# The order of the delta rule planned with TensorE's full-clock durations, and filler products in TensorE's planned gaps

## The chip, the core and the metric

The kernel runs on one core of a Trainium2 chip. The metric is device time in microseconds of one execution, lower is better: 908.51 us for the kernel before, the median of three runs (907.62 to 911.17).

## What is computed

Two blocks follow each other. The first is a delta rule over 4 batches, 8 heads and 768 tokens with a head dimension of 48; its output is reshaped to 3072 tokens of 384 numbers. The second routes each token to two of eight experts by noisy logits, and runs the experts.

```python
    k_n = k / (np.linalg.norm(k, axis=-1, keepdims=True) + 1e-06)
    for t in range(S):
        kt, vt, bt = (k_n[:, :, t], v[:, :, t], beta[:, :, t, None])
        y[:, :, t] = np.einsum('bhd,bhde->bhe', q[:, :, t], state)
        v_old = np.einsum('bhde,bhd->bhe', state, kt)
        state = state + bt[:, :, :, None] * np.einsum('bhd,bhe->bhde', kt, vt - v_old)
...
    noisy_logits = logits + noise_scale * noise
    top2 = np.argpartition(-noisy_logits, 2, axis=1)[:, :2]
...
            h = np.maximum(x[mask] @ w1[e], 0.0)
            out[mask] += top2_w[mask, k, None] * (h @ w2[e])
```

## The kernel before

The delta rule is computed in chunks of 64 tokens (`C`). A unit is one chunk of two batches, so that its 128 rows fill the partitions; there are 12 chunks of 2 units each. Four units (two chunks) make a round, and there are six rounds. In a round the kernel does this, by job:

- `turned` (L477) transposes k and later q of a unit on TensorE, four transposes to a job (L484), and ScalarE copies the result out of PSUM (L491). `products` (L508) then makes the Gram matrix of k (L502, the helper `by_token`), whose diagonal blocks are copied to `gd` (L531) and whose other part to `at` (L537).
- `invert` (L541) inverts the triangular blocks of all units of the round on VectorE: a transposition (L548), row lengths through ScalarE (L555 to L569), the scaling by `low_d` (made by GpSimd, L584, save in the first round), then 30 columns of two dependent instructions each (L599, L603), and the transposed inverses `tb` (L624) and `tt` (L630). It is one long chain of VectorE instructions.
- `join` (L634) puts the 32-wide blocks together on TensorE (L671, L677), with copies on ScalarE (L651, L685, L689).
- `within` (L700) makes the masked product of q and k (L502, then L713 on VectorE).
- `recur` (L720) is the recurrence proper: the state times k (L502, `pair<-st,kT`), subtracted from v on VectorE (L751), solved with the joined inverse (L761), copied by ScalarE (L768), multiplied with k (L779) and added to the state on VectorE (L791). GpSimd scales v (L732) and spreads the state (L804).
- `answer` (L811) makes the outputs (L823, L834), transposes them (L843) and multiplies them with the router's weights (L848). `route` (L894) chooses the experts on VectorE (L906 and around; L955 to L961 count on TensorE, L975 makes the gates, L983 counts), and GpSimd writes each token's row to the rows of its two experts in DRAM (L325).

What sets the order of all this is the class `Jobs`. Each piece of work is a job with an engine and a cost in microseconds, what it reads and writes, and, for TensorE, a PSUM bank that it opens. `order` (L84) first gives every job a due time backwards from its followers, with their costs and 0.15 us for a signal; then it plays the queue of each engine forward in planned time, starting the job that can start first, and among those within 0.05 us of it the one with the earliest due time. A job that opens a bank waits for the earliest empty one (`place`, L105; `empty` holds the planned time at which each bank comes free). The jobs are then emitted in the order of their planned starts; for TensorE, ScalarE, VectorE and SyncE this order is kept as it is. So a cost changes no instruction, only places in the queues. The times of the plan itself exist only while the kernel is built.

`early` (L1073) adds the first part of expert 0's work at the end of the delta rule (L1131, L1157, L1180), as jobs that are taken when nothing else is due. After that the experts run in an order of their own, which no cost touches: the rest of expert 0 (`rest`, L1559) and experts 1 to 7 (L1628, products at L1408).

Of the kernel before, what the change touches and what calls it, by code (L numbers as in the profile page):

```python
# [38 lines left out]
class Jobs:  # L39
# [44 lines left out]
    def order(self):  # L84
        jobs = self.jobs
        for job in reversed(jobs):
            for i in job.after:
                jobs[i].due = min(jobs[i].due, job.due - job.cost - self.SIGNAL)
        for job in jobs:
            job.key = (0, job.due) if job.late is None else (1, job.late)  # L90
        waits = [len(job.after) for job in jobs]
        then = [[] for _ in jobs]
        for job in jobs:
            for i in job.after:
                then[i].append(job.number)
        ready = [0.0] * len(jobs)
        could = [set() for _ in self.ENGINES]
        for job in jobs:
            if not job.after:
                could[job.engine].add(job.number)  # L100
        free = [0.0] * len(self.ENGINES)
        empty = {size: [0.0] * len(x) for size, x in self.banks.items()}
        spaced = moved = 0.0

        def place(size, among):  # L105

            return min(
                ((empty[size][i], i) for i in among if empty[size][i] is not None),
                default=None,
            )  # L110

        done = []
        while len(done) < len(jobs):
            first = {}
            best = None
            for engine in self.ENGINES:
                at = []
                for i in could[engine]:
                    start = max(free[engine], ready[i], spaced if jobs[i].apart else 0.0)
                    if jobs[i].opens:  # L120
                        which = jobs[i].opens.size, jobs[i].opens.among
                        if which not in first:
                            first[which] = place(*which)
                        room = first[which]
                        if room is None:
                            continue
                        start = max(start, room[0])
                    at.append((start, jobs[i].key, i))
                if at:
                    soon = min(at)[0] + self.PATIENCE  # L130
                    pick = min((x for x in at if x[0] <= soon), key=lambda x: x[1:])
                    best = min(best or (1e9,), pick)
            start, _, i = best
            job = jobs[i]
            could[job.engine].remove(i)
            end = free[job.engine] = start + job.cost
            if job.apart:
                spaced = start + job.apart
            if job.opens:
                size, among = job.opens.size, job.opens.among  # L140
                job.opens.at = x = first[size, among][1]
                empty[size][x] = None
                job.opens.tile = self.banks[size][x]
            if job.closes:
                empty[job.closes.size][job.closes.at] = end + self.SIGNAL
            job.start = start
            if job.moves:
                end = moved = max(moved, end) + job.moves
            done.append(job)
            for j in then[i]:  # L150
                ready[j] = max(
                    ready[j],
                    end + (self.SIGNAL + job.lands if jobs[j].engine != job.engine else 0.0),
                )
                waits[j] -= 1
                if not waits[j]:
                    could[jobs[j].engine].add(j)
        return sorted(done, key=lambda job: job.start)

    PATIENCE = 0.05  # L160

    def run(self):
        for job in self.order():
            job.emit()

@with_exitstack
def kernel(
# [39 lines left out]
    nc = tc.nc  # L207
# [165 lines left out]
    def deltanet(ictx):  # L373
# [8 lines left out]
        PE, ACT, DVE, POOL, SP = Jobs.ENGINES  # L382
# [91 lines left out]
        def halves(name, slot):  # L474
            return [(name, slot, i) for i in range(2)]

        def turned(n, name, src, size, to, to_size):  # L477

            p = bank(1, True)

            def emit():
                p_t = p.tile.rearrange("p (j t) -> p j t", t=128)
                for j in range(NP):
                    nc.tensor.transpose(p_t[:, j], src(n)[:, 2 * j : 2 * j + 2], ident)  # L484

            jobs.add(
                PE, 0.75, emit, reads=halves(name, n % size), opens=p,
            )
            jobs.add(
                ACT, 0.6,  # L490
                lambda: nc.scalar.copy(  # L491
                    to(n), p.tile.rearrange("p (j t) -> p j t", t=128)
                ),
                writes=[(name + "T", n % to_size)], closes=p,
            )
# [12 lines left out]
        def products(n):  # L508

            s, i = divmod(n, US)
            turned(n, "k", kps, NK, kTs, NT_)
            p = bank(2, True)
            jobs.add(
                PE, 0.8,
                lambda: by_token(
                    two_banks(p, C), kTs(n), lambda z, j, b: kTs(n)[z, j, rows_of[b]]
                ),  # L520
                reads=[("kT", n % NT_)], opens=p,
            )
            gd = gds.rearrange("p (u j z) i -> p u z j i", u=US, z=2)[:, i]
            for x, lo in enumerate(range(0, 128, Q)):
                rows, cols = slice(lo, lo + Q), slice(lo % C, lo % C + Q)
                on, copy = (DVE, nc.vector.tensor_copy) if s == 0 and x % 2 else (
                    ACT, nc.scalar.copy
                )
                jobs.add(
                    on, 0.38,  # L530
                    lambda rows=rows, cols=cols, copy=copy: copy(  # L531
                        gd[rows], two_banks(p, C)[rows, :, :, cols]
                    ),
                    writes=[("gd", i, lo)], uses=p,
                )
            jobs.add(
                ACT, 0.38, lambda: nc.scalar.copy(ats(n), two_banks(p, C)[:, :, :, Q:C]),  # L537
                writes=[("at", n % NT_)], closes=p,
            )
# [94 lines left out]
        def join(units):  # L634
# [21 lines left out]
            for n, m in zip([*units, None], [None, *units]):  # L656
# [31 lines left out]
                    for up, dn in pairs:  # L688
                        nc.scalar.copy(w64s(m)[up, :, Q:C], p_x()[up])  # L689

                jobs.add(PE, 1.25, products_of, reads=reads, opens=p)
                if n is not None:
                    jobs.add(
                        ACT, 0.8, negated, writes=[("x", n % 2)],
# [5 lines left out]
        def within(n):  # L700

            turned(n, "q", qps, NQ, qTs, NQ)
            p = bank(2, True)
            jobs.add(
                PE, 0.8,
                lambda: by_token(
                    two_banks(p, C), kTs(n), lambda z, j, b: qTs(n)[z, j, rows_of[b]]
                ),
                reads=[("kT", n % NT_), ("qT", n % NQ)], opens=p, lands=2.0,
            )  # L710
            jobs.add(
                DVE, 0.7,
                lambda: nc.vector.tensor_tensor(  # L713
                    out=qks(n), in0=two_banks(p, C),
                    in1=mask[:, None, None, :].to_broadcast([128, 2, NP, C]), op=ALU.mult,
                ),
                writes=[("qk", n % NQ)], closes=p,
            )

        def recur(n):  # L720
# [18 lines left out]
            if c:  # L739
                p_b = bank(2)  # L740
                jobs.add(
                    PE, 0.7,
                    lambda: by_token(
                        two_banks(p_b, D), kTs(n), lambda r, j, b: old[r, b, j]
                    ),
# [17 lines left out]
                            start=(h == 0), stop=(h == H - 1), skip_group_check=True,  # L763
                        )

            jobs.add(PE, 1.3, solve, reads=[*v_key, *every_w], opens=p_u)
            jobs.add(
                ACT, 0.5, lambda: nc.scalar.copy(u_n, per_head(p_u)),  # L768
                writes=[u_key], closes=p_u,
# [5 lines left out]
            def gather_state():  # L775
# [7 lines left out]
                            )  # L783

            jobs.add(
                PE, 0.7, gather_state, reads=[u_key, *halves("k", n % NK)], opens=p_s
            )

            def add_state():
# [21 lines left out]
        def answer(n):  # L811
# [41 lines left out]
            reads = [("qT", n % NQ), ("qk", n % NQ), ("u", n % N_U)]  # L853
            if c:
                reads.append(("wide", z, c % 2))
            jobs.add(PE, 2.2 if c else 1.3, of_chunk, reads=reads, opens=p_y)
            jobs.add(
                ACT, 0.5,
                lambda: nc.scalar.copy(y_n, per_head(p_y).rearrange("p h d -> p (h d)")),
                writes=[y_key], closes=p_y,  # L860
            )
            jobs.add(PE, 0.6, turn, reads=[y_key], opens=p_xt)
            jobs.add(
                ACT, 0.5,
                lambda: nc.scalar.copy(
# [1 line left out]
                ),  # L867
                writes=[xT_key], uses=p_xt,
            )
            jobs.add(PE, 1.0, multiply, reads=[xT_key, "wgn"], uses=p_xt)  # L870
            jobs.add(
                ACT, 0.2,
                lambda: nc.scalar.copy(
# [404 lines left out]
                cut(s, EARLY[s][1] * 128)  # L1278
        for s in EARLY:
            early(s)  # L1280
        with tc.manual_schedule(
            engines={
                mybir.EngineType.PE, mybir.EngineType.Activation, mybir.EngineType.DVE,
                mybir.EngineType.SP,
            }
        ):
            jobs.run()
        return held["w"]

    with ExitStack() as ictx:  # L1290
# [14 lines left out]
    with ExitStack() as ectx:  # L1305
# [322 lines left out]
        for e in range(1, E):  # L1628
# [32 lines left out]
            def run(g, *numbers):  # L1661
                for n in numbers:
                    steps[g][n - 1]()
# [143 lines left out]
```

## Time and profile before

| | us |
|---|---|
| median of three runs | 908.51 |
| the profiled execution | 894.65 |
| its span | 892.8 |
| TensorE busy in the span | 790.1 |
| VectorE busy | 504.7 |
| first inversion starts (L548) | 16.0 |
| first expert product of 512 columns (L1157) | 354.0 |
| last product of the early part of expert 0 (L1180) | 408 |

The profile is of one execution, so durations and places are those of the 894.65 us, not of the median. The page cuts the span into 40 slices; a digit is the busy share of a slice in tenths, and for the line PEclk the granted share of TensorE's full clock. A matmul of float32 appears as two records, one after the other; a transposition as one. Each wait is put down to the event that ended it; "issue" means that the profile shows nothing that the engine waited for.

### The profile page before, as it was taken

The numbers are of one execution on the slowest core, as the hardware profiler recorded it, in microseconds if no ns is written. First come the engines' busy times: TensorE is split into PE (matmuls) and PEld (weight loads), VectorE is DVE, ScalarE is ACT, GpSimd is POOL, SyncE is SP. The second block draws the span as 40 slices with busy tenths as digits, with TensorE's granted clock in tenths as the row PEclk, the third lists the DMA queues.
The fourth block names the chain that finished last, engine by engine and source line by source line (L and its number), as shares of the span: only waits on it lengthen the run. The fifth ranks groups of instructions, "written<-read, shape, count | busy, mean of one in ns | idle before, by whom it ended". The sixth has DMA issues, their size and how long they took to land. (4 is left out here: it accounts for less than half of the span.)

```text
span 892.8 us, 21764 instructions
## 1 busy us (share of the span) xinstructions
PE 790.1 (88%) x9170; PEld 607.4 (68%) x9170; DVE 504.7 (57%) x1210; ACT 311.5 (35%) x743; POOL 321.2 (36%) x331
## 2 busy tenths in 40 slices
PE   4569697697968879999999999999999999999995
PEld 3458585686848767467469578578578587587594
DVE  6968888785898961115465344444455344354342
ACT  3565636628457363201330330320330420420410
POOL 4031144224423323315423634614614515525311
PEclk8657687776976879999999999999999999999998
DMA  4698645451621212633612422423413322301201
GB/s 71 119 312 171 128 92 184 109 156 56 189 73 39 77 45 75 220 105 137 191 66 100 141 73 96 142 72 103 132 71 110 123 71 84 95 10 39 64 20 40
DMA packets 119086, 93.77 MB, mean 105 GB/s; under 512 B 84647, under 2 KB 109256, under 8 KB 118977
## 3 DMA queue, kind: packets, MB, share of 16 engines
q1 hardware_dynamic: 107312, 64.54, 26.5%
q0 software_dynamic: 9552, 27.33, 9.0%
q8 instruction: 74, 1.21, 0.6%
q10 hardware_dynamic: 2112, 0.39, 0.3%
q14 instruction: 36, 0.29, 0.1%
HBM read 58.82 MB, written 34.81 MB: 105 GB/s over the span
## 5 line engine op out<-in xcount | busy, mean ns | idle before, releaser
L367 POOL DMA_INDIRECT out_dram<-sums,index x49 | 48.6, 991 | 161.6 <-DVE sums L1296 138.8
L325 POOL DMA_INDIRECT rows_x<-y,slot x48 | 49.1, 1023 | 109.8 <-DVE t L603 20.0
L1408 PE MATMUL a<-xe,w1e 128*128 128x416 f32 x168 | 69.3, 521 | 0.0
L603 DVE TENSOR_TENSOR t<-t,part 128x30 f32<-128x30 f32 (+9 forms) x180 | 64.4, 358 | 6.2
L599 DVE TENSOR_TENSOR part<-t 128x30 f32<-128x30 f32 (+9 forms) x180 | 61.9, 344 | 5.4
L358 POOL DMA_INDIRECT sums<-out_dram,index x49 | 51.7, 1056 | 34.6 <-issue 24.9
L1478 ACT COPY part_c<-c 128x416 f32<-128x416 f32 x28 | 14.2, 506 | 120.8 <-PE c L1408 120.8
L1408 PEld LDWEIGHTS a<-xe,w1e 128*128 128x128 f32 x168 | 29.6, 189 | 31.4 <-issue 17.8
L1469 DVE TENSOR_TENSOR hT<-part,d 128x416 f32<-128x416 f32 x28 | 16.4, 587 | 57.8 <-ACT part L1486 56.2
L1296 DVE SCALAR_TENSOR_TENSOR sums<-d,gate,sums 128x192 f32<-128x192 f32 x56 | 23.3, 417 | 42.5 <-PE d L1408 42.5
L1463 ACT ACTIVATE hT<-hT 128x416 f32<-128x416 f32 x84 | 45.1, 550 | 4.7 <-DVE hT L1469 2.5
L1445 ACT COPY xe<-x 128x384 f32<-128x384 f32 x21 | 10.1, 479 | 100.1 <-PE x L1440 100.1
L804 POOL COPY wide<-st 64x384 f32<-64x384 f32 x44 | 24.1, 547 | 54.4 <-DVE st L791 30.5
L761 PE MATMUL single<-v,w 64*64 64x48 f32 x768 | 38.3, 269 | 5.3 <-issue 4.0
L1408 PE MATMUL d<-xe,w1e 128*128 128x416 f32 x112 | 41.6, 513 | 0.0
L1408 PE MATMUL c<-xe,s_w 128*128 128x416 f32 x112 | 41.4, 512 | 0.0
L651 ACT COPY w<-tt 32x256 f32<-32x256 f32 x96 | 38.6, 402 | 6.2 <-DVE tt L630 4.3
L761 PEld LDWEIGHTS single<-v,w 64*64 64x64 f32 x768 | 36.3, 187 | 6.4 <-issue 6.2
L484 PE MATMUL single<-ident,kp 128*128 128x128 f32 x96 | 20.4, 350 | 22.5 <-DMA kp<-in_k_dram 13.8
L1469 DVE TENSOR_TENSOR hT<-part,c 128x416 f32<-128x416 f32 x28 | 16.5, 588 | 41.4 <-ACT part L1497 39.9
L1408 PE MATMUL d<-t_w,hT 128*128 128x192 f32 x224 | 38.6, 326 | 0.0
L502 PE MATMUL pair<-st,kT 64*64 64x48 f32 x704 | 19.5, 265 | 21.3 <-DVE st L791 14.0
(242 smaller groups left out, 1889.3 us busy)
## 6 DMA issues: line engine op xcount, KB each, us to landing
w1e<-in_moe_w_dram SPq DMA_DIRECT2D x8, 1536.0 KB
w2e<-in_moe_w_dram SPq DMA_DIRECT2D x8, 1536.0 KB
xr<-rows_x SPq DMA_DIRECT2D x7, 1164.0 KB
rows_x<-empty SPq DMA_DIRECT2D x8, 776.0 KB
v<-in_v_dram SPq DMA_DIRECT2D x48, 96.0 KB
qp<-in_q_dram SPq DMA_DIRECT2D x48, 96.0 KB
out_dram<-empty SPq DMA_DIRECT2D x4, 1152.0 KB
kp<-in_k_dram SPq DMA_DIRECT2D x44, 96.0 KB
```

What stands on the lines that cost most here:

```text
L325: d = nc.gpsimd.indirect_dma_start(out=rows_x, out_offset=bass.IndirectOffsetOnAxis(ap=slot, axis=0), in_=rows, in_offset=None,).ins
L358: nc.gpsimd.indirect_dma_start(out=got, out_offset=None, in_=out, in_offset=bass.IndirectOffsetOnAxis(ap=index, axis=0), bounds_check=N - ...
L367: nc.gpsimd.indirect_dma_start(out=out, out_offset=bass.IndirectOffsetOnAxis(ap=index, axis=0), in_=got, in_offset=None, bounds_check=N - ...
L599: v_.tensor_tensor(out=part, in0=t_inv[:, j + 1 :, j, None].to_broadcast(shape), in1=t_inv[:, None, j, 0:j].to_broadcast(shape), op=ALU.mult,)
L603: latest["column"] = v_.tensor_tensor(out=t_inv[:, j + 1 :, 0:j], in0=t_inv[:, j + 1 :, 0:j], in1=part, op=ALU.add).ins
L651: lambda rows=rows, cols=cols, w64=w64, tt=tt: nc.scalar.copy(w64[rows, :, cols], tt[rows]),
L761: nc.tensor.matmul(per_head(p_u)[b, h], w64[b, h], v_n[b, h], start=(h == 0), stop=(h == H - 1), skip_group_check=True,)
L804: nc.gpsimd.tensor_copy(wide[rows, :, :, y * D : (y + 1) * D], new[rows])
L1296: nc.vector.scalar_tensor_tensor(out=got, in0=p, scalar=gate, in1=got, op0=ALU.mult, op1=ALU.add)
L1408: nc.tensor.matmul(p, lhsT, rhs, start=opens and i == 0, stop=i == len(products) - 1, skip_group_check=True,)
L1463: relu = lambda m, l, src: nc.scalar.activation(hT[:, m, half[l]], src, ACTF.Relu)
L1469: nc.vector.tensor_tensor(out=hT[:, m, half[l]], in0=x, in1=y, op=ALU.add)
```

## The change

The costs of ten kinds of TensorE jobs are lowered, to durations of these products at the full clock. The planner also notes for each job that opens a bank when the planned bank came free (`job.room`). `run` now takes a function `warm`: ahead of a TensorE job that opens a bank, if the plan has TensorE idle for more than 0.5 us after both its previous job and the bank are free, it emits products of the identity with itself into the bank, as many as fit that time at 0.22 us each. The job's own first product starts its accumulation anew, so what they write is not used. The arithmetic of the kernel stays as it was.

```diff
             if job.opens:
                 size, among = job.opens.size, job.opens.among
-                job.opens.at = x = first[size, among][1]
+                job.room, job.opens.at = first[size, among]
+                x = job.opens.at
...
     PATIENCE = 0.05
-
-    def run(self):
+    IDLE, STEP = 0.5, 0.22
+
+    def run(self, warm):
+        free = 0.0
         for job in self.order():
+            if job.engine == self.PE:
+                idle = job.start - max(free, job.room) if job.opens else 0.0
+                free = job.start + job.cost
+                if idle > self.IDLE:
+                    warm(job.opens.tile, int(idle / self.STEP - 0.5))
             job.emit()
...
-                PE, 0.75, emit, reads=halves(name, n % size), opens=p,
+                PE, 0.6, emit, reads=halves(name, n % size), opens=p,
...
-                PE, 0.8,
+                PE, 0.6,
                 lambda: by_token(
                     two_banks(p, C), kTs(n), lambda z, j, b: kTs(n)[z, j, rows_of[b]]
...
-                jobs.add(PE, 1.25, products_of, reads=reads, opens=p)
+                jobs.add(PE, 0.65, products_of, reads=reads, opens=p)
...
-                PE, 0.8,
+                PE, 0.6,
                 lambda: by_token(
                     two_banks(p, C), kTs(n), lambda z, j, b: qTs(n)[z, j, rows_of[b]]
...
-                    PE, 0.7,
+                    PE, 0.5,
                     lambda: by_token(
                         two_banks(p_b, D), kTs(n), lambda r, j, b: old[r, b, j]
...
-            jobs.add(PE, 1.3, solve, reads=[*v_key, *every_w], opens=p_u)
+            jobs.add(PE, 1.1, solve, reads=[*v_key, *every_w], opens=p_u)
...
-                PE, 0.7, gather_state, reads=[u_key, *halves("k", n % NK)], opens=p_s
+                PE, 0.55, gather_state, reads=[u_key, *halves("k", n % NK)], opens=p_s
...
-            jobs.add(PE, 2.2 if c else 1.3, of_chunk, reads=reads, opens=p_y)
+            jobs.add(PE, 1.9 if c else 1.0, of_chunk, reads=reads, opens=p_y)
...
-            jobs.add(PE, 0.6, turn, reads=[y_key], opens=p_xt)
+            jobs.add(PE, 0.45, turn, reads=[y_key], opens=p_xt)
...
-            jobs.add(PE, 1.0, multiply, reads=[xT_key, "wgn"], uses=p_xt)
+            jobs.add(PE, 0.75, multiply, reads=[xT_key, "wgn"], uses=p_xt)
...
+        def warm(bank, times):
+            to = bank if len(bank.shape) == 2 else bank[:, 0]
+            for _ in range(times):
+                nc.tensor.matmul(to[:, 0:128], ident, ident, start=True, stop=True)
+
...
-            jobs.run()
+            jobs.run(warm)
```

## The prediction

> **What bounds the kernel now.** I read the page first, then the windows view cut at the places where VectorE stands still, then VectorE's waits, then the timeline of single products. The page:
>
> ```profile
> span 892.8 us, 21764 instructions
> PE 790.1 (88%) x9170; PEld 607.4 (68%) x9170; DVE 504.7 (57%) x1210; ACT 311.5 (35%) x743; POOL 321.2 (36%) x331
> ...
> PE   4569697697968879999999999999999999999995
> ...
> DVE  6968888785898961115465344444455344354342
> ...
> PEclk8657687776976879999999999999999999999998
> ```
>
> One slice is 22.3 us. From slice 16 (357 us) to the end TensorE is at nine or ten tenths with the full clock: the experts, bound by TensorE. Ahead of that, in the delta rule, VectorE is the busiest (8 to 9 tenths) and the granted clock is 0.5 to 0.9. The change touches only this first part, so it can move the time only by starting the TensorE-bound part earlier or later. The windows view of that part; columns are the stretch, its length, busy time of PE, PEld, DVE, ACT, POOL, granted clock, DMA share, GB/s:
>
> ```profile
> 0.00:16.00 16.00, 7.60 (x144) 5.86 (x144) 9.00 (x47) 7.32 (x16) 9.14 (x35) 0.96 0.39 56
> 16.00:54.90 38.90, 22.47 (x392) 16.98 (x396) 35.49 (x82) 18.70 (x46) 4.34 (x5) 0.59 0.73 155
> 54.90:72.00 17.10, 11.32 (x344) 10.08 (x336) 6.63 (x20) 12.66 (x35) 3.39 (x3) 0.50 0.96 295
> 72.00:107.70 35.70, 28.66 (x783) 25.55 (x784) 33.40 (x87) 19.37 (x52) 5.76 (x9) 0.74 0.82 166
> 107.70:122.40 14.70, 12.30 (x404) 11.45 (x401) 10.24 (x33) 6.98 (x19) 6.01 (x7) 0.73 0.30 57
> 122.40:161.60 39.20, 30.46 (x689) 25.87 (x685) 33.42 (x90) 22.76 (x59) 13.47 (x17) 0.80 0.50 143
> 161.60:198.80 37.20, 31.57 (x807) 29.20 (x807) 31.64 (x89) 14.11 (x37) 9.49 (x12) 0.73 0.52 140
> 198.80:233.10 34.30, 27.70 (x784) 24.34 (x784) 20.10 (x58) 26.17 (x69) 17.57 (x21) 0.70 0.30 80
> 233.10:275.40 42.30, 33.42 (x743) 28.50 (x746) 39.41 (x101) 21.18 (x56) 11.34 (x14) 0.78 0.43 118
> 275.40:317.00 41.60, 35.18 (x938) 31.17 (x930) 37.48 (x101) 19.53 (x51) 17.63 (x22) 0.81 0.25 70
> 317.00:337.80 20.80, 14.64 (x591) 13.76 (x591) 12.93 (x48) 12.64 (x33) 4.24 (x6) 0.75 0.13 42
> 337.80:357.00 19.20, 17.78 (x284) 14.79 (x280) 2.21 (x12) 8.21 (x30) 6.55 (x9) 1.00 0.18 64
> ```
>
> From 16.0 (the first inversion starts) to 337.8 us VectorE is busy 260.7 of 321.8 us. Its work is not changed, so 61 us of idle is all that order and clock can win there; some 18 us of it are gaps of a few tens of ns between dependent small instructions and stay. The other 43 us lie where a round's joins, solves and state products run: 10.5 us of idle at 54.9 to 72, 14.2 at 198.8 to 233.1, 7.9 at the last round, 2 to 6 elsewhere. Those are the stretches with the low clock. The timeline shows what the clock costs one job:
>
> ```profile
> 48.55 1.11 PE L484 MATMUL single<-ident,qp 128*128 128x128 f32 x4
> 199.72 0.66 PE L484 MATMUL single<-ident,kp 128*128 128x128 f32 x4 [0.26 <-ACT logits L873]
> 397.45 5.60 PE L1157 MATMUL pair<-kT,w1e 128*128 128x128 f32 x48 [0.47 <-ACT kT L1143]
> ```
>
> Four transposes take 1.11 us at half clock and 0.66 at full. The old cost of that job, 0.75, lies between; the new 0.6 is the full-clock one. The last row prices a filler: 24 products of 128x128 by 128 columns (two records each) in 5.60 us, 0.233 us apiece at full clock; doubled, 0.467 at half.
>
> [...]
>
> **The change, part by part.**
>
> *New costs.* No product is removed. The planner's TensorE time shrinks, and with it the due times, so 212 of TensorE's 347 jobs and 198 of VectorE's 359 stand elsewhere in their queues, mostly by a few places. The pattern: transposes and Gram products of the next rounds (L484, L502) go ahead of the joins (L671) into the time when TensorE waits for the inverse, and the router's small VectorE jobs (L975, L983) go later, behind masks and sums that TensorE feeds. That aims at rows of VectorE's waits such as these (waiting line, what ended it, us in total, times, longest):
>
> ```profile
> DVE r_den L975 <- ACT r_p L1023: 6.2, 4, 3.2
> DVE v L751 <- issue: 5.7, 2, 3.3
> DVE norm L561 <- ACT root L556: 5.4, 6, 1.7
> DVE v L751 <- PE pair L502: 4.4, 4, 1.7
> DVE t L548 <- ACT gd L531: 2.8, 2, 2.4
> ```
>
> The first and the last can go by order alone; L561 (a ScalarE round trip, 5.4) and the wait for GpSimd's L584 (4.3) cannot. The loads are hardly moved on SyncE's queue; the k rows of round 3, now turned some 40 us earlier, are issued by 91.6 us and wanted near 98, so I cost the earlier use at nothing (if a load were late, TensorE would stand for 2 to 3 us once).
>
> *Fillers.* The order prints 150 in 11 places: 18 at the very start, 30 and 17 before transposes of later rounds, 8, 4, 10, 28, 26 and 5 before joins or the count, 1 and 3 elsewhere. At 0.233 us they are 35 us of TensorE, meant for idle time.
> The 18: the identity is ready at 1.5 us, the first k rows at 4.55. [...] they end at 7.5 to 9.2 us, say 8.4. Then two transposes, the wait of 0.72 and a product take 2.7 us at full clock instead of 4.0, so the first Gram block comes at 11.1 instead of 8.57: +2.5 us (bounds +1.6 and +3.3) on VectorE's first inversion. ScalarE's and VectorE's copies behind it, 7.5 us, stay.
> The 30 and 17: TensorE waits for loads there (5.7 and 3.5 us) while VectorE inverts until 54 us; nothing.
> The 8 and 4 before the first joins: [...] up to 12 x 0.467 = 5.6 us; I take +1.5 of delay. The 10, 28 and 26+5: TensorE stands there waiting for VectorE's transposed inverse (5.6 us at 316); at full clock 28 cost 6.5 us[...]. I take +1 for each of three rounds; bounds 0 and +3.
>
> *Clock.* Half the clock for a share of 2 x (1 - clock) of each window. 54.9 to 72: all of 11.3 us busy at half, so 5.7 us less work; ScalarE with 12.7 of 17.1 busy keeps part, -4. With the +2.5 and +1.5 above the first round comes out at 0. 72 to 107.7: 2.3 of idle, nothing. 107.7 to 122.4: 12.3 x 0.54 / 2 = 3.3 us less work against 4.5 of idle, -1.5. 122.4 to 198.8: the stalls of 3.3 and 2.3 before L751 are TensorE coming late with a state product, half of 5.6, and the waits between, -4. 198.8 to 233.1: 27.7 x 0.6 / 2 = 8.3 us less work and the early Gram products remove the 2.4 us wait at L548; of 14.2 idle, -7. 233.1 to 317: VectorE idles 7.0 of 83.9 us, mostly small gaps, -0.5. 317 to 337.8: 14.6 x 0.5 / 2 = 3.7 less and the 3.2 us wait of L975 moved, -2.5. From 328.8 on the clock is full already: nothing. Sum -15.5; fillers in three later rounds +3; together -12.5. The gains are summed as if each window kept its own; an earlier product often just meets the next wait, on GpSimd (L732, L584) or ScalarE, so I keep three quarters: -9.5 us.
>
> The profiled execution took 894.65 us (span 892.8 and 1.9 around it), so it would be 885.2. The median of the runs shown is 908.51, 13.9 above it; the same difference there gives **899.0 us**.
>
> **The rivals.** (1) *The clock stays full throughout*: the stretches lose their whole PE share, about 24 of the 43 us less 2.5 at the start and some waits on ScalarE: -18, 890.5 us. [...] Against: they fill only gaps that the plan sees ahead of a job that opens a bank, and TensorE's waits for ScalarE copies (0.7 us each, at the transposes) are not among them. (2) *VectorE is the bound and nothing comes of it*: earlier products only move waits to ScalarE and GpSimd; start +2.5, fillers +3, gains 7: -1.5, 907 us. For it: 81% of VectorE busy. Against: the two holes of 10.5 and 14.2 us. (3) *Fillers overrun, slower*: an order made for full-clock products meets a half clock. Each of the 81 fillers before joins and counts costs 0.234 more than its gap; half of them so, 9.5 us, with the 2.5 at the start and the joins now queued behind 4 more transposes (0.45 each, twice): +13 less 3.5 of gain, 918 us. It decides if the clock is still about 0.75 in 50 to 330 us.
>
> **How the numbers follow.** Chances: forecast 0.50 (893 to 904), rival 1 0.17, rival 2 0.14, rival 3 0.19. Within 0.5% (4.5 us, about what a measurement tells from no change) of 908.5 is rival 2. So faster 0.67, same 0.14, slower 0.19. The range 889 to 912 holds the forecast, most of rival 1, rival 2, and the mild end of rival 3.
>
> **What would show it.** Granted clock over 0.85 in 50 to 330 us; the first L548 at 18.5 instead of 16.0; VectorE's idle from there to its last L713 down from 61 to about 47; the first L1157 of 512 columns at about 344 instead of 354; the rest unchanged. Wrong if the joins start late behind fillers that run at 0.467, or if L751's waits stay as long while the clock is high.

## The result, and the profile after

| | before | after |
|---|---|---|
| median, us | 908.07 (906.65 to 911.17, 4 runs) | 931.51 (929.2 to 937.97, 4 runs) |
| ratio, 95% interval | | 1.0265 (1.0206 to 1.0324) |
| the profiled execution | 894.65 | 929.2 |
| first inversion starts (L548) | 16.0 | 18.6 |
| first expert product of 512 columns | 354.0 | 387.0 |
| last product of the early part of expert 0 | 408 | 442 |

The change makes the kernel slower by 2.65%, 23.4 us. The two profiled executions lie 34.6 us apart, since that of the kernel before is 13.4 us below its median; the sums below are from these two and show some 11 us too much. Ratios, here and in the experiments below, leave out the executions that lie more than 1.5% above the fastest of the same kernel: nine of fifteen of `e18_hundredths_down`, two of twenty of `e11_joins_lowered`, three of twenty of `e14_joins_restored`, none elsewhere.

The page of the changed kernel, the same lines as before:

```profile
span 927.5 us, 22352 instructions
PE 828.5 (89%) x9470; PEld 644.5 (69%) x9470; DVE 510.8 (55%) x1210; ACT 311.1 (34%) x743; POOL 320.5 (35%) x331
...
PE   8658878687887887999999999999999999999995
...
DVE  5867578986789782110755435455355354344341
...
PEclk9875669677797878799999999999999999999998
```

One slice is 23.2 us here. The 300 more TensorE instructions are the 150 fillers with two records each. The experts' part, from the last early product to the end, is 485 us in both (892.8 - 407.7 and 927.5 - 442.1). So the whole loss lies in the delta rule. VectorE's digits are lower at most places there, and its last subtraction from v ends 25.4 us later (362.5 after 337.1); the other 7.6 of the 33.0 us by which the first product of 512 columns is late come after it, where two solves took 11.6 us (last section). The clock is no steadier than before. The windows view of the delta rule, cut where VectorE stands still, with the columns of the view shown before:

```profile
18.60:58.00 39.40, 28.57 (x508) 24.50 (x511) 35.67 (x82) 18.44 (x45) 4.33 (x5) 0.87 0.76 165
58.00:86.00 28.00, 18.76 (x592) 17.25 (x592) 16.03 (x41) 17.05 (x46) 6.04 (x7) 0.63 0.88 235
86.00:117.10 31.10, 26.21 (x356) 21.95 (x356) 21.10 (x61) 11.69 (x30) 2.39 (x4) 0.61 0.62 123
...
172.90:198.50 25.60, 21.42 (x701) 19.40 (x701) 20.04 (x51) 14.37 (x37) 12.02 (x15) 0.69 0.41 108
...
```

From 58 to 117 us VectorE works 37.1 of 59.1 us; in the kernel before the stretch from 54.9 to 107.7 had 40.0 of 52.8. Its waits name what it stands for (lines are those of the changed file: L803 and L807 add to the state, L930 is the router's first step, L725 the mask). First the changed kernel, then the same waits in the kernel before (L791, L795, L918):

```profile
DVE r_w L930 <- ACT r_u L927: 16.7, 4, 8.3
DVE st L803 <- PE pair L791: 16.3, 8, 3.2
DVE norm L573 <- ACT root L568: 6.6, 5, 2.7
DVE st L807 <- PE pair L791: 6.0, 2, 5.4
...
DVE v L763 <- PE pair L514: 1.5, 2, 1.3
```

```profile
DVE st L795 <- PE pair L779: 5.3, 2, 4.7
...
DVE r_w L918 <- ACT r_u L915: 1.6, 2, 1.4
...
DVE st L791 <- PE pair L779: 0.4, 1, 0.4
```

The two rows of the kernel before that the prediction wanted gone are gone: no wait for the gates (`r_den`) is left, and the waits before the subtraction from v have shrunk. Summed over VectorE's gaps of more than 0.15 us between the first inversion and the last subtraction, the gaps before v, `r_den`, `r_at` and t fell from 24.7 to 2.9 us. But those before the state's additions, the router's first steps (`r_w`) and the masks rose from 7.8 to 46.2. The gaps as a whole went from 43.0 to 59.5 us, VectorE's busy time in the stretch from 260.1 to 266.7 with the same instructions, and the stretch from 321.1 to 343.9. (Why they last longer stayed open. It goes with the order: in the last pair of experiments it is 260.9 in the old one and 267.3 in the new.) How a state's addition comes late is seen in the timeline of the third round (starts, durations, TensorE and then VectorE; the joins' products of 32x32 lie between these rows):

```profile
172.03 0.64 PE L967 MATMUL single<-r_taken,mask_u 128*128 128x32 f32 x2 [0.86 <-ACT x L697]
...
176.64 1.14 PE L514 MATMUL pair<-qT,kT 64*64 64x64 f32 x32 [1.23 <-DVE v L763]
...
179.27 1.14 PE L514 MATMUL pair<-qT,kT 64*64 64x64 f32 x32 [0.49 <-DVE qk L725]
...
183.81 1.83 PE L773 MATMUL single<-v,w 64*64 64x48 f32 x29
...
185.51 1.13 PE L514 MATMUL pair<-qT,kT 64*64 64x64 f32 x30
186.43 1.89 PE L773 MATMUL single<-v,w 64*64 64x48 f32 x32
189.04 1.41 PE L791 MATMUL pair<-u,kp 64*64 64x48 f32 x64
...
189.82 0.56 DVE L803 TENSOR_TENSOR st<-pair,st 128x384 f32<-128x384 f32 x1 [3.19 <-PE pair L791]
```

A product for a mask has gone in before each of the next joins and between the two solves. The costs say 0.6 us for it and 1.1 for a solve; it took 1.13, and the solves 1.83 and 1.89 (the granted clock from 172.03 to 189.04 us was 0.51). ScalarE's copy of the first solve started at 185.83 and took 0.48, so the state product could have started at 186.3; it started at 189.04, behind a mask, the second solve and a join, and VectorE stood for 3.19 us. In the plan the same piece, from the count (L967) to the state product, takes 12.9 us; it took 17.0 (172.03 to 189.04). In the old order this piece is shorter, and it keeps its plan: 10.2 us planned, 10.8 measured (L955 to L779).

```profile
161.07 0.41 PE L955 MATMUL single<-r_taken,mask_u 128*128 128x32 f32 x2 [1.59 <-ACT w L689]
...
171.90 1.15 PE L779 MATMUL pair<-u,kp 64*64 64x48 f32 x64
```

### The profile page after: what moved, and what is told of

It reads as the page before. It is cut to its first block, busy times and chain, and to the rows that moved or that the text cites. A ratio compares the mean times of both kernels' runs of the same rounds, so it can differ in the third digit from the quotient of the medians.

```text
span 927.5 us, 22352 instructions
## 1 busy us (share of the span) xinstructions
PE 828.5 (89%) x9470; PEld 644.5 (69%) x9470; DVE 510.8 (55%) x1210; ACT 311.1 (34%) x743; POOL 320.5 (35%) x331
## 3 DMA queue, kind: packets, MB, share of 16 engines
q8 instruction: 76, 1.25, 0.6%
## 5 line engine op out<-in xcount | busy, mean ns | idle before, releaser
L337 POOL DMA_INDIRECT rows_x<-y,slot x48 | 47.2, 984 | 111.1 <-DVE t L615 42.0
L615 DVE TENSOR_TENSOR t<-t,part 128x30 f32<-128x30 f32 (+9 forms) x180 | 67.0, 372 | 6.2
L370 POOL DMA_INDIRECT sums<-out_dram,index x49 | 52.1, 1064 | 35.5 <-issue 24.7
L773 PE MATMUL single<-v,w 64*64 64x48 f32 x768 | 40.2, 263 | 17.8 <-issue 14.2
L816 POOL COPY wide<-st 64x384 f32<-64x384 f32 x44 | 24.7, 562 | 72.6 <-DVE st L803 54.7
L1313 DVE SCALAR_TENSOR_TENSOR sums<-d,gate,sums 128x192 f32<-128x192 f32 x56 | 23.4, 417 | 42.5 <-PE d L1425 42.5
L1296 PE MATMUL single<-ident 128*128 128x128 f32 x292 | 38.4, 295 | 3.1 <-POOL ident masks.py:199 1.5
L663 ACT COPY w<-tt 32x256 f32<-32x256 f32 x96 | 38.6, 402 | 4.9 <-DVE tt L642 1.7
L1296 PEld LDWEIGHTS single<-ident 128*128 128x128 f32 x292 | 37.0, 209 | 3.7 <-POOL ident masks.py:199 1.5
L1425 PE MATMUL d<-t_w,hT 128*128 128x192 f32 x224 | 38.6, 326 | 0.0
```

Source lines behind the costliest of these rows:

```text
L337: d = nc.gpsimd.indirect_dma_start(out=rows_x, out_offset=bass.IndirectOffsetOnAxis(ap=slot, axis=0), in_=rows, in_offset=None,).ins
L370: nc.gpsimd.indirect_dma_start(out=got, out_offset=None, in_=out, in_offset=bass.IndirectOffsetOnAxis(ap=index, axis=0), bounds_check=N - ...
L615: latest["column"] = v_.tensor_tensor(out=t_inv[:, j + 1 :, 0:j], in0=t_inv[:, j + 1 :, 0:j], in1=part, op=ALU.add).ins
L663: lambda rows=rows, cols=cols, w64=w64, tt=tt: nc.scalar.copy(w64[rows, :, cols], tt[rows]),
L773: nc.tensor.matmul(per_head(p_u)[b, h], w64[b, h], v_n[b, h], start=(h == 0), stop=(h == H - 1), skip_group_check=True,)
L816: nc.gpsimd.tensor_copy(wide[rows, :, :, y * D : (y + 1) * D], new[rows])
```

## The experiments

The kernel before takes 895 us on some chips and 907 to 909 on others, so each ratio below is to the kernel before on the same chip, and only ratios are compared. Letters in the expectations name theories as described beside them.

### The order, the fillers, and single costs

`e1_order_only` is the changed kernel without fillers; `e2_fill_only` is the kernel before, with its costs and order, and 82 fillers in the gaps of that plan.

```diff
 e1
-                if idle > self.IDLE:
-                    warm(job.opens.tile, int(idle / self.STEP - 0.5))
 e2
+                if idle > self.IDLE:
+                    warm(job.opens.tile, int(idle / self.STEP - 0.5))
...
```

> The changed order, with all 150 fillers left out. If the order made for full-clock products is what costs (VectorE's queue holds the router's first instructions ahead of the end of the inversion, and waits there for answers that are late), this is as slow as the changed kernel or slower, 928 to 940 us, and VectorE's wait for r_u at the second inversion stays at 6 us or more. If the fillers are what costs, it comes back to 900 to 912 us.

> The old costs and so exactly the old order of all jobs, with the fillers that this plan's own gaps ask for (82 instead of 150). If the order is what costs, this is within 4 us of the kernel before (904 to 912 us). If fillers hold products back, it is slower by 0.23 to 0.47 us for each that lies on the path: 920 us or more.

Measured: order alone 1.0182 (1.0121 to 1.0243), fillers alone 0.9997 (0.9982 to 1.0013). VectorE's waits for the state in the first are those of the changed kernel:

```profile
DVE st L801 <- PE pair L789: 17.0, 8, 3.2
DVE st L805 <- PE pair L789: 6.4, 2, 4.8
```

So the order carries the loss, and the fillers in the old order come to nothing. In the new order they may cost up to some 0.8% more (1.0265 against 1.0182, intervals that overlap). The two also repeat the comparison of the gaps on one chip: those before v, `r_den`, `r_at` and t are 28.3 us in e2 and 10.5 in e1, those before the state's additions, the router's first steps and the masks 8.7 and 38.6. The router's wait that e1 was expected to keep at 6 us or more is 2.6 at most. `e3_answers_restored` takes back three of the ten costs in the changed kernel, those of the answers; `e4_route_late` tells the planner of the changed kernel that the router's first ScalarE job lands 8 us later, so that the router's VectorE job stands further back in the queue.

```diff
 e3
-            jobs.add(PE, 1.9 if c else 1.0, of_chunk, reads=reads, opens=p_y)
+            jobs.add(PE, 2.2 if c else 1.3, of_chunk, reads=reads, opens=p_y)
...
 e4
-                ACT, 0.5, small_exp, reads=every_logit, writes=["r_u"]
+                ACT, 0.5, small_exp, reads=every_logit, writes=["r_u"],
+                lands=easy(8.0),
```

> The changed kernel with only the costs of the answers put back (of_chunk 2.2 and 1.3, turn 0.6, multiply 1.0); this asks for 83 fillers, and puts the router's rounding (L920 of the kernel before) behind the last column in two of five rounds instead of none. Order theory: the wait of 8 us in round 1 goes and half of the loss comes back, 912 to 922 us. Filler theory: the fillers at the start and before the first joins, 77 of them, are the same, so 920 us or more. If the loss is in the state products' order it stays at 928.

> The changed kernel with the plan alone told that the router's first ScalarE result lands 8 us later, so that VectorE's rounding stands behind the last column in four of five rounds; full-clock costs and 104 fillers stay. Order theory: most of the loss comes back, 905 to 916 us, and no wait of VectorE for r_u is over 2 us. Filler theory: 922 us or more.

Measured: 1.0071 (1.0045 to 1.0096) and 1.0195 (1.0131 to 1.0259). The router's wait of 8.3 us, the longest of all, is not what the loss rests on: without it e1 lost 1.8%, and e4, which should have won most of the loss back if this wait made it, lost 1.95%. Told of it, the planner moved it, and VectorE waited elsewhere, for TensorE before v and one step later in the router:

```profile
DVE v L763 <- PE pair L514: 18.5, 10, 6.1
DVE r_w L918 <- ACT r_w L1021: 16.0, 4, 6.4
```

### Costs the other way, and many more fillers

`e5_half_costs` is the kernel before with costs for half the clock (transposition 1.05, join 1.15, solve 1.9, outputs 3.4). `e8_answers_lowered` is the kernel before with the answers' three costs alone lowered as in the change. `e9_spare_after` and `e10_spare_before` put fillers into every planned gap over 0.1 us, in unused columns of an empty pair of banks: 269 in the changed order, 205 in the old.

```diff
 e5
-            jobs.add(PE, 1.3, solve, reads=[*v_key, *every_w], opens=p_u)
+            jobs.add(PE, 1.9, solve, reads=[*v_key, *every_w], opens=p_u)
...
 e8
-            jobs.add(PE, 2.2 if c else 1.3, of_chunk, reads=reads, opens=p_y)
+            jobs.add(PE, 1.9 if c else 1.0, of_chunk, reads=reads, opens=p_y)
...
 e9 (in e10 the added lines alone)
-                if idle > self.IDLE:
-                    warm(job.opens.tile, int(idle / self.STEP - 0.5))
+                if job.late is None and job.spare is not None and job.idle > 0.1:
+                    warm(job.spare, int(1.0 * job.idle / 0.233 + 0.3))
```

> The kernel before with TensorE's costs raised to the half-clock durations of its own profile (transposes 1.05, L502 1.05, joins 1.15, solve 1.9, L779 1.1, answers 3.4 and 1.9, turn 0.85, router product 1.3), no fillers. If the loss comes from a plan that believes in products faster than they are, a plan that believes in slow ones is no worse than before, 895 to 910 us, with VectorE's waits for the state sums and the router under 10 us together. If any change of order away from the tuned one loses, 915 us or more.

> The kernel before with only the answers' three costs lowered, as the change lowers them, no fillers. If the answers' costs alone carry what restoring them took away (some 15 of 23 us), this is 919 to 927 us; if they hurt only together with the other lowered costs, 907 to 913 us.

> The changed order with 269 fillers instead of 150: every planned idle stretch of TensorE over 0.1 us in which the plan has one of the three pairs of banks empty, written to columns of that pair that no job uses. If the order would be good at the full clock and only the clock is missing, the clock in 50 to 340 us goes over 0.85 and the time falls below 915 us. If the order loses for another reason (ScalarE's copies between products, waits for loads), the clock rises and the time stays at 922 us or more; and if fillers now overrun, it passes 935 us.

> The old costs and old order with 205 fillers placed in the same way. If the clock is worth something to the old order, it is 895 to 905 us, below both kernels; if the old order is bound by VectorE and the clock is worth nothing, 905 to 912 us; if fillers overrun, 915 us or more.

Measured: e5 1.0337 (1.0308 to 1.0365), e8 0.9865 (0.9848 to 0.9881), e9 1.0195 (1.0162 to 1.0227), e10 1.0032 (1.0014 to 1.0051). The clock of e10 and of e2 from 50 to 330 us was 0.80 and 0.77, against 0.73 in the kernel before, and neither became faster; e9, with 0.81, lost as much as the new order without fillers. Either a higher clock gives nothing here and fillers cost nothing, or the two cancel; they were not separated. e8, a part of the change, beats both kernels. Costs that fit the half clock, expected to be no worse than before, do still worse than the changed ones: an order is not better for being made with slower products either.

### Which queue, which cost, or chance

`e16_hold_vector` and `e17_hold_tensor` have the changed costs, no fillers, and one part of the old order written out as a list of jobs: VectorE's queue, or TensorE's and ScalarE's. `e18_hundredths_down` lowers four costs of before by 0.02 us, `e11_joins_lowered` the join alone.

```diff
 e16, e17
+                    if engine in held and i != held[engine][at_of[engine]]:
+                        continue
 e18
-                PE, 0.75, emit, reads=halves(name, n % size), opens=p,
+                PE, 0.73, emit, reads=halves(name, n % size), opens=p,
...
 e11
-                jobs.add(PE, 1.25, products_of, reads=reads, opens=p)
+                jobs.add(PE, 0.65, products_of, reads=reads, opens=p)
```

> The changed costs, no fillers, but VectorE's queue held instruction for instruction as before; TensorE's and ScalarE's queues follow the changed costs (208 of TensorE's 347 jobs stand elsewhere than before). Theory A (the loss is made by VectorE's own queue, in which the router's block and the masks stand at other places): ratio 0.99 to 1.005. Theory B (the loss is made by TensorE's queue, where masked products and transpositions stand ahead of solves and state products, and VectorE only waits for it): 1.012 to 1.025.

> The changed costs, no fillers, but TensorE's and ScalarE's queues held exactly as before; only VectorE's queue follows the changed costs (150 of its 359 jobs stand elsewhere). Theory A (VectorE's own queue makes the loss): ratio 1.012 to 1.025. Theory B (TensorE's queue makes it): 0.99 to 1.005. If both this and the run with VectorE's queue held come out near 1.00, it is the two queues together.

> The kernel before with four costs lowered by 0.02 us each (transposition 0.73, join 1.23, solve 1.28, state product 0.68), no fillers; 139 of TensorE's jobs and 145 of VectorE's change places all the same. Theory C (the loss comes of costs that are too low): 0.02 us is nothing, ratio 0.997 to 1.003. Theory D (the planner answers any disturbance with another order, good or bad by chance): away from 1 by 0.5 to 2% on either side.

> The kernel before with the join's cost alone lowered from 1.25 to 0.65 us, no fillers. Theory C (a cost that is too low does the harm, and the join's is the one lowered most): 1.012 to 1.025. Theory D (any disturbance gives another order by chance): anywhere between 0.985 and 1.03, which tells little if it is high, and speaks against C if it is 1.00 or below.

Measured: 1.0322 (1.0269 to 1.0375), 1.0265 (1.0218 to 1.0311), 0.9981 (0.995 to 1.0012), 0.9991 (0.9967 to 1.0014). Neither queue by itself is the fault; with one of them as before the loss is no smaller. A low cost of the join alone does no harm, and a disturbance that moves 139 of TensorE's jobs and 145 of VectorE's changes the time by some 0.5% at most: its ratio rests on six executions, and the median of all fifteen, 912.8 us, is 0.5% above the kernel before. So chance alone is a poor explanation too, as far as one such order can tell.

What was left came from laying each plan beside its execution. Planned and measured start of the transposed inverse `tb`, by round, and of the last subtraction from v:

| us | `tb`, round 1 | 3 | 5 | last v |
|---|---|---|---|---|
| before: planned | 89.6 | 192.4 | 302.3 | 325.9 |
| measured | 95.5 | 202.3 | 312.3 | 336.6 |
| order alone (e1): planned | 90.4 | 195.2 | 295.6 | 314.4 |
| measured | 101.9 | 219.6 | 338.8 | 360.6 |

(Rounds counted from 0.) The old order runs 10 us behind its plan; in e2, on the same chip as e1, its last v comes at 341.4, 15.5 behind. The new one promises 11.5 us less than the old and falls 46 behind, some at every round. The planner knows durations only through its costs. I replayed the planned orders by the planner's own rules, queues and banks kept, first with every TensorE cost of the delta rule at its full-clock value, then half way from it to the half-clock value. From the first to the second the old order loses 20 us (from 350.1 to 370.6 for its last job on VectorE, the early part of expert 0 left out), the new one 53 (from 339.1 to 392.0). Over the thirteen orders measured apart from the searched one below (two of them, e3 and e4, with fillers), the rank correlation of the half-way end with the measured ratio is 0.93. It is 0.64 for the full-clock end and 0.65 for one three quarters of the way, so it hangs on that choice. Ten of them were known when the replay was made, so it needed new orders.

### The replay put to the test

`e14_joins_restored` is the changed kernel without fillers and with the join's cost back at 1.25. `e12_recurrence_lowered` is the kernel before with three costs lowered. `e20_fifth_of_half` has all costs a fifth of the way from full to half clock. `e19_searched` has costs chosen by a search for an early end in the replay.

```diff
 e14
-                jobs.add(PE, 0.65, products_of, reads=reads, opens=p)
+                jobs.add(PE, 1.25, products_of, reads=reads, opens=p)
 e12
-            jobs.add(PE, 1.3, solve, reads=[*v_key, *every_w], opens=p_u)
+            jobs.add(PE, 1.1, solve, reads=[*v_key, *every_w], opens=p_u)
...
-                PE, 0.7, gather_state, reads=[u_key, *halves("k", n % NK)], opens=p_s
+                PE, 0.55, gather_state, reads=[u_key, *halves("k", n % NK)], opens=p_s
...
 e20
-            jobs.add(PE, 1.3, solve, reads=[*v_key, *every_w], opens=p_u)
+            jobs.add(PE, 1.26, solve, reads=[*v_key, *every_w], opens=p_u)
...
 e19
-            jobs.add(PE, 1.3, solve, reads=[*v_key, *every_w], opens=p_u)
+            jobs.add(PE, 1.01, solve, reads=[*v_key, *every_w], opens=p_u)
...
-            jobs.add(PE, 0.6, turn, reads=[y_key], opens=p_xt)
+            jobs.add(PE, 0.87, turn, reads=[y_key], opens=p_xt)
...
```

> The changed kernel without fillers and with the join's cost put back from 0.65 to 1.25 us; the other nine costs stay low. Theory E (an order laid out for products at the full clock is too tight for what runs: where TensorE needs longer than the costs say, masked products and transpositions that fitted a planned gap hold back the solves behind them). Replaying the planned orders with every TensorE cost half way from the full-clock to the half-clock value ends the last VectorE job at 370.6 for the order before, 392.0 for the changed one, 383.6 for this one: 13 us more than before, ratio about 1.014. Theory D (chance): no relation to the replay, 0.985 to 1.03. Theory C (the join's low cost does the harm): about 1.00.

> The kernel before with the recurrence's costs alone lowered (state times k 0.5, solve 1.1, state product 0.55), no fillers. Theory E: replayed with half-way costs it ends at 367.0 against 370.6 before, so ratio about 0.996 (0.985 to 1.003). Theory D (chance): no relation to the replay, up to 1.03. Theory C (low costs by themselves do harm): 1.01 or more.

> All eleven costs set a fifth of the way from the full-clock to the half-clock duration (join 0.75, solve 1.26, transposition 0.69), no fillers. Theory E: replayed with half-way costs it ends at 382.3, 11.7 us behind the order before, ratio about 1.013, between before (1.00) and the changed order (1.018). Theory D (chance): no relation, anywhere from 0.985 to 1.03.

> The kernel before with its eleven costs chosen by a search so that the planned order, replayed with TensorE a quarter, a half and three quarters of the way to half-clock durations, ends early (337.8, 354.1, 383.7; the order before 353.6, 370.6, 401.4); no fillers. Theory E: 16 us earlier, ratio about 0.982, and at least below 0.992. Theory D (chance): the replay tells nothing, so about 1.00 with a spread of 0.985 to 1.03.

Measured: e14 1.0036 (1.0015 to 1.0057), e12 0.9885 (0.9852 to 0.9918), e20 1.0048 (1.0025 to 1.0071), e19 1.0036 (1.0021 to 1.0051). The signs of the first three are as forecast, but the two losses are about a third of what the replay said, and the gain of e12, 10 us, is nearly three times it. The searched order is a miss: 16 us promised, none come. Its last subtraction came at about 336 us, not far from that of the kernel before (337), and its first product of 512 columns at 360 instead of 354. So the replay sorted orders that were made without it, and what was picked by it brought nothing. And taking back either the join's cost or the answers' costs regains over half of the loss, though neither does harm alone: the harm needs several costs low together.

### The same two orders with short products

The last pair takes the duration itself away. All small products of the delta rule read the upper halves of their float32 operands as bfloat16, so each is one record instead of two (TensorE has 5,986 records in both runs, 9,170 in the kernel before; a solve of 16 records took 0.62 us in e22); the output is therefore a rounded one. `e21_thin_before` has the costs and queues of before, `e22_thin_after` those of the change, without fillers.

```diff
+        def thin(out, a, b, **marks):
+            high = lambda x: x.bitcast(mybir.dt.bfloat16)[..., 1::2]
+            nc.tensor.matmul(out, high(a), high(b), **marks)
```

> The order before, with all small products of the delta rule (Gram, masks, joins, state times k, solve, state product, outputs) taken from the upper halves of their float32 operands as bfloat16, one pass instead of two records each, so these TensorE jobs are much shorter; the values are rounded, so the routing, and with it the experts' part, can differ a little. Costs, and so the queues, are those of before. It is the base for the next run: 10 to 30 us less than before in the delta rule.

> The changed order without fillers, with the same short products. Theory E (the order is too tight for TensorE's actual durations): with jobs shorter than the costs its plan holds, and it ends before the order before with the same products; replayed with these jobs at 0.3 to 0.5 of their costs it is 9 us ahead, so the ratio of this run to the one before it about 0.99 (below 1.00). Theory F (the order is bad whatever TensorE needs, by its places in VectorE's and ScalarE's queues): it stays 12 to 18 us behind, ratio of the two about 1.015 to 1.02.

Measured against the kernel before: e21 0.9734 (0.971 to 0.9758), e22 0.9676 (0.9659 to 0.9693). The medians are 885.11 and 878.52 us: with short products the changed order is the faster one, by 6.6 us, where with full ones it was 1.8% slower. Pages of e21 and of e22:

```profile
span 883.6 us, 15369 instructions
...
DVE  6979887995999932007544345355444454354342
...
PEclk9999555555555556999999999999999999999998
```

```profile
span 877.3 us, 15349 instructions
...
DVE  6979899998999822016554344454454454354441
...
PEclk9999999999999999999999999999999999999998
```

VectorE's waits for the state in e22:

```profile
DVE st L805 <- PE pair L509: 3.9, 2, 2.2
```

The waits of 23.4 us in e1 have become 3.9, and the plan is kept: the last subtraction was planned at 314.4 and came at 317.8 (in e21 planned at 325.9, at 323.6). An order bad by its places alone would have stayed 12 to 18 us behind. So the loss comes of TensorE's jobs taking longer than the costs on which this order is laid out.

The clock of e21's profile is at half from 50 us to 330 (0.56 in that window) and that of e22 at full (1.00), but the 6.6 us are not the clock's. Over a whole execution e21 had a mean clock of 0.848 in the profiled one (885.37 us) and of 0.992 to 0.996 in the four others (880.78 to 885.2), and e22 of 0.85 in one (878.52) and 0.996 to 0.997 in four (878.21 to 879.1). With products this short the clock made no difference that these times show, in either order. One rival is only bounded: short products are also half as many records, and TensorE's waits for nothing that the profile shows, between 16 and 336 us, are 13.8 us in the kernel before, 19.1 in e1, 8.3 in e21 and 5.0 in e22. So some 5 us of the loss may be of that kind, not the whole.

## Why the prediction was wrong

- **What bounds it, and the unchanged part**: right. The loss is in the delta rule alone, and the experts took 485 us as before.
- **Start, +2.5 us**: right, and by the path named; the first fillers ended at 8.7 us (forecast 8.4) and the first L548 came at 18.6 (18.5). The first fourteen took 6.14 us, 0.44 each, and the last four, from 7.67 us on, started 0.22 apart; the prediction reckoned with 0.467 and 0.233. Without fillers it came at 16.6, so 2.0 of it are theirs.
- ***New costs***: this is the step that failed. It costed the new places of 212 TensorE and 198 VectorE jobs as waits removed ("The first and the last can go by order alone") and set nothing against them. The named waits did go (24.7 to 2.9 us). But masks that were moved forward stand in TensorE's queue ahead of joins, solves and state products, as in the third round above, and VectorE waits in the state's additions and the router (7.8 to 46.2 us). Order alone measured +1.8%; the term was taken as a gain.
- ***Clock*, -15.5 and with fillers -12.5, three quarters kept**: wrong. The clock from 50 to 330 us was 0.77, not over 0.85; in the kernel before 0.73. Where fillers raised it to 0.80 in the old order, the time did not fall (1.0032). That the new order and the fillers would bring the full clock was the author's estimate. The prediction took the low clock for the reason of VectorE's idle time, but its own table speaks against that: from 16.0 to 54.9 us the clock was 0.59, and VectorE idled 3.4 of 38.9 us. In the trace of the kernel before, from 14.7 to 328.8 us, the clock went 13 times from 1.0 to 0.5 and 13 times back, in stretches of 3.41 us and multiples of it (up to 44.37). TensorE was busy for 0.2 to 2.1 of the 3.41 us ahead of each fall (1.35 ahead of the one at 257.1), and for 3.0 to 3.4 of the 3.41 us ahead of each rise; but it was so from 72.77 to 76.18 too (3.41), and the clock stayed at 0.5.
- ***Fillers* +1.5, and +1 for each of three rounds**: not shown apart from the clock; in the old order the two together came to nothing (0.9997).
- **Marks**: VectorE's idle to its last mask is 72 us (335.8 less 263.6), not 47; the first L1157 of 512 columns came at 387, not 344.
- **Rivals**: the third had the sign, "an order made for full-clock products meets a half clock", and its point of decision, a clock of about 0.75, was met. But it charged 9.5 of its 13 us to fillers that overrun, and its sum was 9.5 us net where 23.4 were measured. The experiments put the charge on the order itself.

The margin showed in what was already quoted: four transpositions at 1.11 us against a cost of 0.6, in stretches with a clock of 0.5 to 0.8. I used that pair of numbers only to price what a faster clock would give, not to ask what the new plan does if the clock stays.

## What to carry to other kernels

A cost in a planner that only sets an order is not a duration to be measured at its best. Lower costs let it fill small gaps with work that nobody waits for, and each such piece holds back the chain behind it in the queue when products are slower (in the third round a state product that could have started at 186.3 us started at 189.04). Before an order is changed, lay the plan beside the trace of the present one, and replay the new order with the durations that the trace shows in that stage; but test what it picks, since a search by such a replay brought nothing here. Changing one group of costs at a time (the answers' alone: 0.9865; the recurrence's alone: 0.9885) found better orders than changing all ten.

## What the runs showed of the hardware

TensorE stands still at times where the profile shows nothing that it waits for. In the kernel before it did so for 3.57 us, next to a burst of loads at 175 us and within the products of the state with k (starts and durations):

```profile
174.26 1.07 PE L502 MATMUL pair<-st,kT 64*64 64x48 f32 x57 [0.59 <-DVE st L791]
178.90 0.35 PE L502 MATMUL pair<-st,kT 64*64 64x48 f32 x4 [3.57 <-issue]
```

In 175 to 180 us its DMA view has 2,275 packets on the loads' queue and one on the instruction queue; what held TensorE there was not shown. And while GpSimd wrote rows in eight indirect DMAs, one behind the other, TensorE crawled through two solves. In the changed kernel (GpSimd, then TensorE):

```profile
362.43 0.98 POOL L337 DMA_INDIRECT rows_x<-y,slot  x1 [0.86 <-POOL wide L816]
363.71 0.96 POOL L337 DMA_INDIRECT rows_x<-y,slot  x1 [0.30 <-issue]
...
364.51 0.38 PE L773 MATMUL single<-v,w 64*64 64x48 f32 x6 [0.38 <-issue]
...
366.73 1.02 PE L773 MATMUL single<-v,w 64*64 64x48 f32 x5 [1.11 <-issue]
```

These last two solves, 3.7 us for two at half clock in the third round, lasted from 363.35 to 374.95. In e1 they took 10.7 us at the same place. But the writes alone don't do it. In e9, with the same order, eight of them in a row ran from 356.61 to 366.45, and both solves took 2.04 us:

```profile
356.61 0.98 POOL L343 DMA_INDIRECT rows_x<-y,slot  x1 [0.86 <-POOL wide L822]
...
357.87 2.04 PE L779 MATMUL single<-v,w 64*64 64x48 f32 x64
```

What else held TensorE up in the changed kernel and in e1 stayed open.
